# First layers of four experts made as filler and sent through memory, and all eight second layers by seven products, in an attention and expert-mixture kernel

## The chip, the cores and the metric

The kernel runs on one core of one Trainium2 chip. Its time is in device microseconds (us) of that core, and a time without further word is the median of several runs. A profiled execution has a time of its own, and its trace has a span, from the first to the last instruction, that is a little shorter. The names of the engines are PE (TensorE, matmuls), PEld (its weight loads), DVE (VectorE), ACT (ScalarE), POOL (GpSimd) and SP (SyncE, which here issues DMA transfers). SBUF is the memory on the chip that all engines work from, PSUM the small memory that matmuls write to, and DRAM stands for the large memory outside the core.

## The reference, cut to what matters

```python
# attention: 8 batches, 8 heads, 512 local and 32 global tokens, head size 64
out_g = softmax(scale * q_g @ [k_g, k_l].T) @ [v_g, v_l]
s_l   = [scale * q_l @ k_g.T, where(|i - j| <= 32, scale * q_l @ k_l.T, -1e9)]
out_l = softmax(s_l) @ [v_g, v_l]
x = concat(out_g, out_l)              # 8 * 544 = 4352 tokens, 8 * 64 = 512 columns

# routing: E = 8 experts, w_gate 512 x 8
P = exp(x @ w_gate - max)
for _ in range(8):
    P /= P.sum(1) + 1e-9              # rows
    P /= P.sum(0) + 1e-9              # columns
    P *= N / E

# experts: w1[e] 512 x 1024, w2[e] 1024 x 512; every token goes through every expert
out = sum(P[:, e:e+1] * (maximum(x @ w1[e], 0) @ w2[e]) for e in range(8))
```

The inputs and the output are fp32. P is positive, so an expert's P may be multiplied into x ahead of the first layer, into h (the result of the first layer) or into the output: the result is the same.

## The kernel before

**Tokens and groups.** The tokens stand in nine groups: m = 0 to 7 are the 512 local tokens of a batch each, m = 8 the 256 global tokens of all batches. `xT` holds the attention's output in SBUF, transposed (512 columns as 4 tiles of 128 partitions, 4352 tokens, fp16). An expert's first layer on a group is 8 blocks (FT) of 4 matmuls each, 32 matmuls of 512 columns. An expert on a group of 512 is called a unit here.

**Order.** The schedule is written out by hand: each engine does its instructions in the order in which the code issues them, and semaphores between the engines follow from the tiles. A pool with n buffers lets a new tile start when the tile n before it has been read for the last time.

**Attention.** There are 32 steps s, one for a pair of heads of a batch, worked in stages that overlap from step to step: `st_A` transposes q and k, `st_B` makes scores (L296, L298), adds the mask on DVE with its row maximum (L303) and takes the exponential on ACT (L306); `st_N` normalises (L342 and L343 on DVE, L347 on POOL), `st_D1` and `st_D2` transpose the weights (L354, L364), and `st_E` multiplies by v and copies the result into `xT` (L381). The global rows go through `st_G0` to `st_G3` in every other step; `st_G3` ends with two copies into `xT`, one on ACT and one on DVE (both L440). POOL casts q and k to fp16 (L127 for example).

**Filler.** Between these stages PE is given matmuls of experts 0 and 1. `f1(eng)` issues one first-layer block (`p_l1`: 4 matmuls, L459) and its eviction through ReLU, by ACT (L462) or DVE (L464), as `eng` says "a" or "v". `f2(eng)` issues one of the four parts of a second layer (`p_l2`: 8 matmuls, L473), its eviction (L476), and after the last one stores the unit's result y to DRAM (`yd`, L480, on ACT's queue). Both write to PSUM pool `ps_mm`, which has two buffers. A unit of group m may start at step 4m + 5. In a step from 9 on there are, in this order, two `f1("a")`, `f2("a")`, `f1("v")`, `f2("a")` and `f1("v")`, with the attention's stages between them.

**Routing.** After the last step come the routing iterations: `sk_rows` and `sk_cols` on DVE (among others two multiplications each through the helper `tt`, L698) with a sum over the partitions on PE, and filler (`tail_run`) behind each. `spread_p` then turns columns 2 to 7 of P into rows and stores them to DRAM (`pd`), from where they are loaded as `pb`, one expert's P for a group, the same on all partitions.

**Expert loop.** For each group m and each e of 2 to 7 (`egs`), `load_w1` brings w1 as fp16 (1 MB, two buffers, SP's queue, L718), `load_pb` brings pb (L725), and `scale_x` makes `xs` = x * P on DVE (L698, 128x2048). `l1` makes h (matmuls L762, eviction with ReLU on ACT L764). The second layer is done by Strassen's method for two-by-two blocks, seven products in place of eight. `prep_w2c` makes the sums of w2 blocks once for an expert: five DVE operations of 128x1024. `sums` makes those of h for each unit: one DVE operation of 128x2048 into `s` and three of 128x1024, two of them in place in `h` (L698). `product` issues products 1 to 7 of 8 matmuls of 256 columns (L798). Products 1 to 5 stay in PSUM for all experts of a group (`ps_fix`), and products 6 and 7 take a rotating buffer and are added into `o` at once (L804, DVE); after a group's last expert the five fixed ones are added too. Within one turn of the loop, PE does the products of unit i and the first layer of unit i + 1 in alternation:

```python
        for fm in range(3):
            l1(i + 1, fm, ps_rot, "r")
        for q, fm in ((3, 3), (4, 4), (5, 5), (2, 6), (1, 7), (6, None), (7, None)):
            ...
            product(i, q)
            if fm is not None:
                l1(i + 1, fm, ps_rot, "r")
```

Experts 0 and 1 come in through `load_y` (o and y1 from `yd`) and `init_o`, which multiplies them by their columns of P, four ACT operations (L750) and four DVE operations (L751) a group. The very last unit has a second layer of its own (`last_pair`, L823). `store` writes o to the output.

Of the kernel before, what the change touches and what calls it, by code (L numbers as in the profile page):

```python
# [23 lines left out]
def kernel(  # L24
# [39 lines left out]
    xT = persist.tile([P, DP, NTOK], FP16)  # L64
# [5 lines left out]
    hpool = ctx.enter_context(tc.tile_pool(name="hpool", bufs=2))  # L70
    ypool = ctx.enter_context(tc.tile_pool(name="ypool", bufs=2))
    ydram = ctx.enter_context(tc.tile_pool(name="ydram", bufs=1, space=DRAM))
    yd = [[ydram.tile([P, NJ if m < B else NT - GT0, D], FP32, name=f"yd{e}_{m}") for m in range(B + 1)]
          for e in range(2)]
    w1d = [ydram.tile([P, DP, F], FP16, name=f"w1d{e}") for e in range(2, E)]
    pd = ydram.tile([E - 2, NTOK], FP32, name="pd")

    groups = [(512 * m, 512) for m in range(B)] + [(512 * B, NTOK - 512 * B)]

# [8 lines left out]
    with tc.tile_pool(name="att_c", bufs=1) as att_c, \  # L88
# [44 lines left out]
        def load_vrow(b):  # L133
            f = vraw[b] = wpool.tile([P, H, NJ, Dh], FP32, tag="w2e", name="vraw")
            for g in range(2):
                nc.sync.dma_start(out=f[:, 4 * g : 4 * g + 4].rearrange("p h s d -> p h (s d)"),
                                  in_=v_l[b, 4 * g : 4 * g + 4].rearrange("h (p s) d -> p h (s d)", s=NJ))
# [76 lines left out]
        qgf = ypool.tile([P, H, NJ * Dh], FP32, tag="y", name="qgf")  # L214
# [151 lines left out]
        def st_E(n):  # L366
# [14 lines left out]
            cp(out=xT[:, hp, Sl * b : Sl * (b + 1)], in_=po)  # L381
# [44 lines left out]
        def st_G3(b, g):  # L426
# [10 lines left out]
            t0 = GT0 * P + Sg * b  # L437
            for a, cp in ((0, nc.scalar.copy), (1, nc.vector.tensor_copy)):
                r = slice(HB * a, HB * (a + 1))
                cp(out=xT[r, 2 * g : 2 * g + 2, t0 : t0 + Sg], in_=po[r, :, Sg * a : Sg * (a + 1)])  # L440

        def logits(t0, nt):
            pl = ps_mm.tile([P, 512], FP32, tag="mm")
            for t in range(nt):
                for dk in range(DP):
                    nc.tensor.matmul(pl[:, E * t : E * (t + 1)], xT[:, dk, P * (t0 + t) : P * (t0 + t + 1)],
# [3 lines left out]
        hTs, ysts, wts = {}, {}, {}  # L450

        def p_l1(e, m, fm, eng, pool=None, tag="mm"):
            c0, n = groups[m]
# [4 lines left out]
            for dk in range(DP):  # L458
                nc.tensor.matmul(ph[:, 0:n], wts[e][0][:, dk, P * fm : P * (fm + 1)], xT[:, dk, c0 : c0 + n],  # L459
# [5 lines left out]

        def p_l2(e, m, c, eng, pool=None, tag="mm"):
            nt = groups[m][1] // P
            if c == 0:
                ysts[(e, m)] = ypool.tile([P, NJ, D], FP32, tag="y", name="yst")
            hT, ys = hTs[(e, m)], ysts[(e, m)]  # L470
            py = (pool or ps_mm).tile([P, D], FP32, tag=tag, name="py")
            for fk in range(FT):
                nc.tensor.matmul(py, hT[:, fk, P * c : P * (c + 1)], wts[e][1][:, fk, :],  # L473
                                 start=(fk == 0), stop=(fk == FT - 1))
            if eng == "a":
                nc.scalar.copy(out=ys[:, c, :], in_=py)  # L476
            else:
                nc.vector.tensor_copy(out=ys[:, c, :], in_=py)
            if c == nt - 1:
                nc.scalar.dma_start(out=yd[e][m], in_=ys[:, 0:nt, :])  # L480

        def load_w1e(e):
            wts[e] = [wpool.tile([P, DP, F], FP16, tag="w1e", name="w1e"), None]
            nc.gpsimd.dma_start(out=wts[e][0], in_=moe_w1[e].rearrange("(dko dki) f -> dki dko f", dki=P))

        def load_w1d(e):
            nc.gpsimd.dma_start(out=w1d[e - 2], in_=moe_w1[e].rearrange("(dko dki) f -> dki dko f", dki=P))

        def load_w2e(e):
            wts[e][1] = wpool.tile([P, FT, D], FP16, tag="w2e", name="w2e")  # L490
            nc.gpsimd.dma_start(out=wts[e][1], in_=moe_w2[e].rearrange("(fko fki) d -> fki fko d", fki=P))

        fill = [(k % 2, k // 2) for k in range(2 * (B + 1))]
        n1 = n2 = 0
# [481 lines left out]
```

## Time and profile before

| | |
|---|---|
| median of three runs | 1062.13 us (1061.54 to 1063.48) |
| profiled execution, its own time | 1065.03 us |
| its span | 1063.3 us, mean granted TensorE clock 0.994 |
| PE busy | 1033.2 us, 97% of the span |
| DVE busy | 689.0 us, 65% |
| ACT busy | 550.3 us, 52% |
| POOL busy | 138.2 us, 13% |
| chain that ended last | PE 78%, ACT 11%, DVE 7%, DMA 2% |
| DMA | 160.57 MB, mean 151 GB/s |

The page of the profile gives the busy time of each engine, its share in each of 40 equal slices of the span (a digit is tenths), the chain of work that ended last, and the costliest groups of instructions: line, engine, operation, output and input tiles with their shapes, how many, then busy time and the mean of one in ns, and the idle time ahead of them with what ended it. The trace answers for a stretch of time or for single shapes in the same manner. A line of the timeline is start, duration, engine, line, operation, tiles, number of instructions, and in brackets the engine's wait ahead of it. Durations in the trace are those of one profiled execution.

### The profile page before, as it was taken

The page shows a single profiled execution, that of the slowest core. Times are in us where ns is not written, and L with a number is a line of the kernel's source. Part 1 is how long each engine was busy: PE and PEld are TensorE (multiplying, and loading weights), DVE is VectorE, ACT ScalarE, POOL GpSimd, SP SyncE. Part 2 cuts the span into 40 slices and gives each one's busy share as a digit, 9 for nine tenths or more (in the row PEclk, how much of TensorE's full clock was granted, in tenths as well). Part 3 has the DMA queues.
Part 4 walks back from the last instruction along what each step waited for, and adds up shares of the span by engine and source line. Part 5 has one row for each costly group of instructions (what it writes and reads, how often), then busy time and mean ns, then how long its engine had stood idle before and what let it go on. Part 6 is the DMA issues. An engine that isn't in the chain of part 4 may idle for free.

```text
span 1063.3 us, 20825 instructions
## 1 busy us (share of the span) xinstructions
PE 1033.2 (97%) x8444; PEld 662.8 (62%) x8444; DVE 689.0 (65%) x1443; ACT 550.3 (52%) x1340; POOL 138.2 (13%) x224
## 2 busy tenths in 40 slices
PE   7889999999999999999999999999999999999997
PEld 3555555555555456666666666666666666666686
DVE  7677667767774748776576576475484484484484
ACT  6777877878775554343343343343343343343342
POOL 6443333323414200000000000000000000000000
PEclk9999999999999999999999999999999999999999
DMA  9945786768637964534524424425326226225243
GB/s 259 213 91 150 126 205 158 124 199 166 110 99 151 234 241 156 186 111 144 187 99 141 177 100 167 151 99 191 126 100 216 101 100 218 100 100 180 93 156 117
DMA packets 95799, 160.57 MB, mean 151 GB/s; under 512 B 32716, under 2 KB 68696, under 8 KB 84696
## 3 DMA queue, kind: packets, MB, share of 16 engines
q1 hardware_dynamic: 45208, 119.98, 33.7%
q0 software_dynamic: 46736, 20.20, 15.5%
q10 hardware_dynamic: 3760, 19.07, 4.5%
q8 instruction: 66, 1.08, 0.4%
q14 instruction: 29, 0.24, 0.1%
HBM read 149.24 MB, written 33.40 MB: 172 GB/s over the span
## 4 chain that ended last, share of the span: by engine, by line
PE 78%; ACT 11%; DVE 7%; DMA 2%; issue 1%; POOL 0%; SPq 0%; ACTq 0%; DVEq 0%
PE ph L762 33%; PE m L798 20%; PE pm L798 8%; PE ph L459 6%; PE py L473 6%; ACT Pu L306 4%; ACT qbd L280 1%; ACT hT L462 1%; DVE Pu L343 1%; ACT Pg L407 1%; DVE m L404 1%; PE pv L151 1%; DMA pb<-pd 1%; DMA vraw<-in_v_l_dram 1%; ACT yst L476 1%
## 5 line engine op out<-in xcount | busy, mean ns | idle before, releaser
L764 ACT ACTIVATE h<-ph 128x512 f16<-128x512 f32 (+1 forms) x432 | 247.1, 573 | 395.3 <-PE ph L762 390.4
L762 PE MATMUL ph<-xs,w1s 128*128 128x512 f16 (+1 forms) x1728 | 405.2, 367 | 1.4 <-ACT h L764 0.5
L762 PEld LDWEIGHTS <-w1s 128*128 128x128 f16 x1728 | 169.0, 98 | 125.8 <-issue 2.6
L804 DVE SCALAR_TENSOR_TENSOR o<-pm,o 128x512 f32<-128x512 f32 (+1 forms) x106 | 70.5, 666 | 241.0 <-PE pm L798 240.7
L798 PEld LDWEIGHTS <-h 128*128 128x128 f16 x1616 | 158.1, 98 | 48.4
L798 PE MATMUL m<-w2c,s 128*128 128x256 f16 x1212 | 158.3, 273 | 0.0
L798 PEld LDWEIGHTS <-s 128*128 128x128 f16 x1212 | 118.6, 98 | 43.8
L459 PE MATMUL ph<-xT,w1e 128*128 128x512 f16 (+1 forms) x576 | 136.5, 371 | 0.0
L473 PE MATMUL py<-w2e,hT 128*128 128x512 f16 x544 | 128.4, 379 | 0.1
L698 DVE TENSOR_TENSOR xs<-xT,pb 128x2048 f16<-128x2048 f16 (+2 forms) x57 | 117.3, 2062 | 9.2 <-DMA pb<-pd 9.2
L798 PE MATMUL m<-w2c,h 128*128 128x256 f16 x808 | 105.5, 273 | 0.0
L798 PE MATMUL pm<-w2c,h 128*128 128x256 f16 x808 | 96.9, 273 | 0.0
L306 ACT ACTIVATE Pu<-ms,mx 128x160 f16<-128x160 f32 x224 | 93.6, 420 | 3.5 <-DVE mx L303 1.6
L698 DVE TENSOR_TENSOR s<-h 128x2048 f16<-128x2048 f16 (+1 forms) x106 | 92.3, 912 | 4.5 <-ACT h L764 4.5
L459 PEld LDWEIGHTS <-w1e 128*128 128x128 f16 x576 | 54.5, 100 | 48.7 <-issue 2.4
L473 PEld LDWEIGHTS <-hT 128*128 128x128 f16 x544 | 49.5, 97 | 51.3 <-issue 0.2
L303 DVE CUSTOM_DVE_ANT_0 ms<-sc,mask 128x160 f32<-128x160 f32 x224 | 60.1, 320 | 23.2 <-PE sc L298 21.8
L698 DVE TENSOR_TENSOR h<-h 128x1024 f16<-128x1024 f16 (+1 forms) x106 | 65.6, 661 | 0.0
L462 ACT ACTIVATE hT<-ph 128x512 f16<-128x512 f32 (+1 forms) x91 | 48.4, 557 | 32.4 <-PE ph L459 31.5
L804 DVE SCALAR_TENSOR_TENSOR o<-m,o 128x512 f32<-128x512 f32 (+1 forms) x90 | 52.2, 655 | 0.3
L476 ACT COPY yst<-py 128x512 f32<-128x512 f32 x68 | 39.4, 580 | 23.1 <-PE py L473 20.9
L347 POOL TENSOR_TENSOR Pl<-Pu,rs 128x256 f16<-128x256 f16 x32 | 24.2, 757 | 189.8 <-PE ph L459 53.0
(154 smaller groups left out, 1007.3 us busy)
## 6 DMA issues: line engine op xcount, KB each, us to landing
w1s<-w1d SPq DMA_DIRECT2D x54, 1024.0 KB
yd<-yst ACTq DMA_DIRECT2D x16, 1024.0 KB
pb<-pd SPq DMA_DIRECT2D x48, 256.0 KB
o<-yd SPq DMA_DIRECT2D x8, 1024.0 KB
y<-yd SPq DMA_DIRECT2D x8, 1024.0 KB
out_dram<-o SPq DMA_DIRECT2D x8, 1024.0 KB
f<-in_q_l_dram SPq DMA_DIRECT2D x15, 512.0 KB
f<-in_k_l_dram SPq DMA_DIRECT2D x15, 512.0 KB
```

The source lines that it names most:

```text
L303: nc.vector.tensor_tensor_reduce(out=ms[:, ii, :], in0=sc[:, SW * ii : SW * (ii + 1)], in1=mask[:, mi, :], scale=-scale, scalar=BIG, op0=A ...
L306: nc.scalar.activation(out=d["Pu"][:, i, :], in_=ms[:, ii, :], func=AF.Exp, scale=-1.0, bias=d["mx"][:, i : i + 1], accum_out=d["sm"][:, i ...
L347: nc.gpsimd.tensor_tensor(out=d["Pl"], in0=d["Pu"][:, :, KW:SW], in1=d["rs"].unsqueeze(2).to_broadcast([P, NHB, Sg]), op=ALU.mult)
L459: nc.tensor.matmul(ph[:, 0:n], wts[e][0][:, dk, P * fm : P * (fm + 1)], xT[:, dk, c0 : c0 + n], start=(dk == 0), stop=(dk == DP - 1))
L462: nc.scalar.activation(out=hT[:, fm, 0:n], in_=ph[:, 0:n], func=AF.Relu)
L473: nc.tensor.matmul(py, hT[:, fk, P * c : P * (c + 1)], wts[e][1][:, fk, :], start=(fk == 0), stop=(fk == FT - 1))
L476: nc.scalar.copy(out=ys[:, c, :], in_=py)
L698: nc.vector.tensor_tensor(out=out, in0=in0, in1=in1, op=op)
L762: nc.tensor.matmul(ph[:, 0:n], w1s[i][:, dk, P * fm : P * (fm + 1)], xss[i][:, dk, 0:n], start=(dk == 0), stop=(dk == DP - 1))
L764: nc.scalar.activation(out=hs[i][:, fm, 0:n], in_=ph[:, 0:n], func=AF.Relu)
L798: nc.tensor.matmul(pm[:, HD * t : HD * (t + 1)], lhs[0][:, k, lhs[1] + P * t : lhs[1] + P * (t + 1)], w[:, q - 1, k, :], start=(k == 0 and ...
L804: nc.vector.scalar_tensor_tensor(out=o, in0=pm[:, 0 : HD * nt].rearrange("p (t d) -> p t d", d=HD), scalar=sg / float(E), in1=o, op0=ALU.m ...
```

## The change

The filler makes only first layers, those of experts 0 to 3, and stores each h to DRAM (`hd`) by SP's queue. The expert loop runs over all eight experts of a group in the order 4, 0, 5, 1, 6, 2, 7, 3: an expert from 4 on is computed as before (x scaled by P on DVE, first layer, ReLU), one below 4 is loaded (`load_h`) and its h multiplied by P on POOL (`scale_h`, 128x4096 in one operation). All eight second layers go through the products. `yd`, `load_y` and `init_o` go.

Around that, `xT` becomes one tile for each group in a pool of its own, stored to DRAM (`xd`) and given back after the filler; the loop loads x for a group again (`load_x`). In the freed space the w2 blocks of experts 7 and 3 and one of the two `s` tiles are placed, so their loads are issued only after the filler. POOL prepares the w2 blocks of experts 0 to 3, DVE those of 4 to 7. `hpool` goes from 2 to 4 buffers, `ypool` from 2 to 1. `spread_p` spreads all eight columns. Each quarter of o is started by an ACT multiplication, two of them at the group's first expert and two at its end. Of the loop, a turn of even i holds the products of computed unit i with the first layer of unit i + 2 between them, and a turn of odd i the products of loaded unit i alone.

```diff
-    xT = persist.tile([P, DP, NTOK], FP16)
...
-    hpool = ctx.enter_context(tc.tile_pool(name="hpool", bufs=2))
-    ypool = ctx.enter_context(tc.tile_pool(name="ypool", bufs=2))
+    hpool = ctx.enter_context(tc.tile_pool(name="hpool", bufs=4))
+    ypool = ctx.enter_context(tc.tile_pool(name="ypool", bufs=1))
...
+    NL = E // 2
+    hd = [[ydram.tile([P, FT, n], FP16, name=f"hd{e}_{m}") for m, (_, n) in enumerate(groups)] for e in range(NL)]
+    xd = [ydram.tile([P, DP, n], FP16, name=f"xd{m}") for m, (_, n) in enumerate(groups)]
+    w1d = [ydram.tile([P, DP, F], FP16, name=f"w1d{e}") for e in range(NL, E)]
+    pd = ydram.tile([E, NTOK], FP32, name="pd")
+    psx = ExitStack()
+    xpool = psx.enter_context(tc.tile_pool(name="xpool", bufs=1, side="right"))
+    xT = [xpool.tile([P, DP, n], FP16, name=f"xT{m}") for m, (_, n) in enumerate(groups)]
...
-            cp(out=xT[:, hp, Sl * b : Sl * (b + 1)], in_=po)
+            cp(out=xT[b][:, hp, :], in_=po)
+            if hp == HP - 1:
+                nc.sync.dma_start(out=xd[b], in_=xT[b])
...
-                cp(out=xT[r, 2 * g : 2 * g + 2, t0 : t0 + Sg], in_=po[r, :, Sg * a : Sg * (a + 1)])
+                cp(out=xT[B][r, 2 * g : 2 * g + 2, t0 : t0 + Sg], in_=po[r, :, Sg * a : Sg * (a + 1)])
+            if b == B - 1 and g == 1:
+                nc.sync.dma_start(out=xd[B], in_=xT[B])
...
         def p_l1(e, m, fm, eng, pool=None, tag="mm"):
...
-                nc.tensor.matmul(ph[:, 0:n], wts[e][0][:, dk, P * fm : P * (fm + 1)], xT[:, dk, c0 : c0 + n],
+                nc.tensor.matmul(ph[:, 0:n], wts[e][:, dk, P * fm : P * (fm + 1)], xT[m][:, dk, :],
...
             if eng == "a":
                 nc.scalar.activation(out=hT[:, fm, 0:n], in_=ph[:, 0:n], func=AF.Relu)
             else:
                 nc.vector.tensor_scalar(out=hT[:, fm, 0:n], in0=ph[:, 0:n], scalar1=0.0, scalar2=None, op0=ALU.max)
+            if fm == FT - 1:
+                nc.sync.dma_start(out=hd[e][m], in_=hT[:, :, 0:n])
...
-        fill = [(k % 2, k // 2) for k in range(2 * (B + 1))]
+        fill = [(k % NL, k // NL) for k in range(NL * (B + 1))]
...
+        def f1(engs, **kw):
             nonlocal n1
-            k, fm = divmod(n1, FT)
-            if not f1_ready():
-                return 0
-            p_l1(*fill[k], fm, eng, **kw)
-            n1 += 1
-            return 1 if fill[k][1] < B else 0.5
-
-        def f2(eng, **kw):
-            nonlocal n2
-            k, c = divmod(n2, NJ)
-            need = FT * (k + 1)
-            if k >= len(fill) or n1 < need or (n1 == need and f1_ready()):
-                return 0
-            nt = groups[fill[k][1]][1] // P
-            p_l2(*fill[k], c, eng, **kw)
-            n2 += 1 if c + 1 < nt else NJ - c
-            return 2
+            v = 0
+            for eng in engs:
+                k, fm = divmod(n1, FT)
+                if k < len(fill) and slot >= HP * fill[k][1] + 5:
+                    p_l1(*fill[k], fm, eng, **kw)
+                    n1 += 1
+                    v += 1 if fill[k][1] < B else 0.5
+            return v
...
-            f1("a")
-            f1("a")
+            f1("aa")
...
             if s < NU:
                 st_B(s, 1)
-            f2("a")
+            if s > HP:
+                f1("va")
             if s + 1 < NU:
                 st_A(s + 1)
             f1("v")
...
-            f2("a")
+            if s > HP:
+                f1("va")
...
             if s > 2 * HP:
                 f1("v")
...
-    w2c = [wc.tile([P, 7, FT // 2, D // 2], FP16, name=f"w2c{e}") for e in range(2, E)]
-    y1 = wc.tile([P, NJ, D], FP32, name="y1")
+    ORDER = (4, 0, 5, 1, 6, 2, 7, 3)
+    w2c = {e: wc.tile([P, 7, FT // 2, D // 2], FP16, name=f"w2c{e}") for e in ORDER[:6]}
...
-    for e in range(2, E):
     def prep_w2c(e):
+        w = w2c[e]
+        eng = nc.gpsimd if e < NL else nc.vector
+        tt(w[:, 0], w[:, 1], w[:, 4], ALU.add, eng)
+        tt(w[:, 5], w[:, 1], w[:, 2], ALU.add, eng)
+        tt(w[:, 6], w[:, 3], w[:, 4], ALU.add, eng)
+        tt(w[:, 2], w[:, 2], w[:, 4], ALU.subtract, eng)
+        tt(w[:, 3], w[:, 3], w[:, 1], ALU.subtract, eng)
+
+    for e in ORDER[:6]:
         load_w2c(e)
...
+    def load_x(m):
+        if m <= B:
+            xgs[m] = xsp.tile([P, DP, 512], FP16, tag="xg", name="xg")
+            nc.sync.dma_start(out=xgs[m][:, :, 0 : groups[m][1]], in_=xd[m])
...
+    def alloc_h(i):
+        if i < NUN:
+            hs[i] = hpool.tile([P, FT, 512], FP16, tag="hT", name="h")
+
+    def load_h(i):
+        if i < NUN:
+            m, e = units[i]
+            alloc_h(i)
+            nc.sync.dma_start(out=hs[i][:, :, 0 : groups[m][1]], in_=hd[e][m])
+
+    def scale_h(i):
+        if i < NUN:
+            n = groups[units[i][0]][1]
+            h = hs[i][:, :, 0:n]
+            tt(h, h, pbs.pop(i)[:, 0:n].unsqueeze(1).to_broadcast([P, FT, n]), ALU.mult, nc.gpsimd)
...
-        s = ss[i] = wpool.tile([P, 3, HF, 256], FP16, tag="w2e", name="s")
+        s = ss[i] = (wpool.tile([P, 3, HF, 256], FP16, tag="w2e", name="s", bufs=1) if i % 2 else
+                     wr.tile([P, 3, HF, 256], FP16, tag="s", name="s"))
...
+    def closes(i):
+        m, e = units[i]
+        return e == (ORDER[-1] if m < B else ORDER[-2])
...
+    def add(i, q, pm):
+        m, e = units[i]
+        nt = groups[m][1] // P // 2
+        if m not in os_:
+            os_[m] = ypool.tile([P, NJ, D], FP32, tag="y", name="o")
+        for j, (r, d, sg) in enumerate(QUARTER[q]):
+            o = os_[m][:, nt * r : nt * (r + 1), HD * d : HD * (d + 1)]
+            p = pm[:, 0 : HD * nt].rearrange("p (t d) -> p t d", d=HD)
+            if (q >= 6 and e == ORDER[0]) or (q in (3, 4) and j == 0):
+                nc.scalar.mul(o, p, 1.0 / float(E))
+            else:
+                nc.vector.scalar_tensor_tensor(out=o, in0=p, scalar=sg / float(E), in1=o, op0=ALU.mult, op1=ALU.add)
...
+        pt = ps_po.tile([P, 3, P], FP32, tag="po", name="pt")
+        pts = xsp.tile([3 * NT, 3, P], FP32, tag="xs", name="pts")
+        parts = [(k, 3 * k, min(3 * k + 3, E)) for k in (1, 0, 2)]
+        for k, e0, e1 in parts:
+            nc.tensor.matmul(pt[0 : (e1 - e0) * NT, k, :], lt[:, e0:e1, :], idf, start=True, stop=True)
+            nc.scalar.mul(pts[0 : (e1 - e0) * NT, k], pt[0 : (e1 - e0) * NT, k], float(E))
+            nc.sync.dma_start(out=pd[e0:e1].rearrange("e (t p) -> (e t) p", p=P), in_=pts[0 : (e1 - e0) * NT, k, :])
...
+    load_pb(0)
+    load_x(0)
     load_w1(0)
-    load_pb(0)
     load_pb(1)
-    prep_w2c(2)
-    prep_w2c(3)
+    prep_w2c(4)
+    prep_w2c(0)
+    prep_w2c(1)
     scale_x(0)
-    scale_x(1)
+    load_pb(2)
+    scale_x(2)
     tail_run(1000)
-    load_w1(1)
-    load_pb(2)
-    load_y(0)
+    load_w1(2)
+    psx.close()
+    wr = ctx.enter_context(tc.tile_pool(name="wr", bufs=1, side="right", reuse_waits="tile"))
+    for e in ORDER[6:]:
+        w2c[e] = wr.tile([P, 7, FT // 2, D // 2], FP16, name=f"w2c{e}")
+        load_w2c(e)
+    alloc_h(0)
+    load_h(1)
+    scale_h(1)
     for fm in range(FT):
         pool, tag = cyc[fm % 2]
         l1(0, fm, pool, tag)
+    sums(0)
...
+    for i, (m, e) in enumerate(units):
+        if i == NUN - 1:
             last_pair(i)
-            break
-        sums(i)
-        if e == 2 and i > 0:
-            init_o(m)
-        scale_x(i + 2)
-        if m == 0 and e + 2 < E:
-            prep_w2c(e + 2)
-        for fm in range(3):
-            l1(i + 1, fm, ps_rot, "r")
-        for q, fm in ((3, 3), (4, 4), (5, 5), (2, 6), (1, 7), (6, None), (7, None)):
-            if i == 0 and q == 2:
-                init_o(m)
-            product(i, q)
-            if fm is not None:
-                l1(i + 1, fm, ps_rot, "r")
+        elif i % 2 == 0:
+            alloc_h(i + 2)
+            load_pb(i + 3)
+            load_pb(i + 4)
+            if (i + 4) % E == 0:
+                load_x((i + 4) // E)
+            load_h(i + 3)
+            load_w1(i + 4)
+            scale_h(i + 3)
+            for fm in range(3):
+                l1(i + 2, fm, ps_rot, "r")
+            for q, fm in ((3, 3), (4, 4), (5, 5), (2, 6), (1, 7), (6, None), (7, None)):
+                product(i, q)
+                if fm is not None:
+                    l1(i + 2, fm, ps_rot, "r")
+                if q == 3:
+                    if i + 2 < NUN:
+                        sums(i + 1)
+                    else:
+                        n = groups[m][1]
+                        h = hs[i + 1]
+                        s = ss[i + 1] = wpool.tile([P, HF, n], FP16, tag="w2e", name="sl", bufs=1)
+                        tt(s, h[:, 0:HF, 0:n], h[:, HF:FT, 0:n], ALU.add)
+                if q == 4:
+                    scale_x(i + 4)
+                if q == 5 and m == 0 and i + 2 < E:
+                    prep_w2c(units[i + 2][1])
+                    if i + 3 > 3:
+                        prep_w2c(units[i + 3][1])
+            if closes(i):
+                for q in (3, 4, 5, 2, 1):
+                    add(i, q, fixed[q])
+        else:
+            if i + 1 < NUN:
+                sums(i + 1)
+            for q in (3, 4, 5, 2, 1, 6, 7):
+                product(i, q)
+                if closes(i) and q in (3, 4):
+                    add(i, q, fixed[q])
+            if closes(i):
+                for q in (5, 2, 1):
+                    add(i, q, fixed[q])
+                store(m)
```

## Prediction, written before the result was known

> **What bounds the kernel now.** I read the page's busy table first, then the chain of waits in the last two thirds, the groups by shape, and the timeline of single steps of the first third.
>
> The page:
>
> ```profile
> PE 1033.2 (97%) x8444; PEld 662.8 (62%) x8444; DVE 689.0 (65%) x1443; ACT 550.3 (52%) x1340; POOL 138.2 (13%) x224
> ...
> POOL 6443333323414200000000000000000000000000
> ```
>
> TensorE (PE) never rests for long, and POOL does nothing after the first third. The chain of waits inside the expert loop (start, us, what):
>
> ```profile
> 448.58 1.75 PE pm L798 x16
> 450.33 2.59 PE ph L762 x12
> 452.92 0.87 PE m L798 x8
> 453.79 0.86 PE ph L762 x4
> ...
> 461.60 1.75 PE pm L798 x16
> ```
>
> One unit (an expert on 512 tokens) takes 461.60 - 448.58 = 13.02 us and the chain is PE alone. A 512-column matmul costs 2.59 / 12 = 0.216 us, a 256-column one 0.875 / 8 = 0.109 us: first layer 32 x 0.216 = 6.91, second layer 7 products x 0.875 = 6.12. So the loop is bound by PE and only matmuls taken away shorten it, as long as everything else stays hidden.
>
> The groups by shape (busy, mean ns) give VectorE's (DVE's) prices:
>
> ```profile
> L698 DVE TENSOR_TENSOR xs<-xT,pb 128x2048 f16<-128x2048 f16 x47 | 107.5, 2286 | 0.4 <-DMA pb<-pd 0.4
> L804 DVE SCALAR_TENSOR_TENSOR o<-pm,o 128x512 f32<-128x512 f32 x96 | 66.3, 691 | 231.1 <-PE pm L798 231.0
> L698 DVE TENSOR_TENSOR h<-h 128x1024 f16<-128x1024 f16 x96 | 61.8, 686 | 0.0
> L698 DVE TENSOR_TENSOR s<-h 128x2048 f16<-128x2048 f16 x48 | 58.3, 1215 | 4.5 <-ACT h L764 4.5
> L464 DVE TENSOR_SCALAR hT<-ph 128x512 f16<-128x512 f32 x53 | 36.6, 691 | 16.6 <-PE ph L459 16.2
> ```
>
> The timeline of DVE and POOL near the start:
>
> ```profile
> 22.55 0.96 DVE L343 TENSOR_TENSOR Pu<-Pu,rs 128x768 f16<-128x768 f16 x1
> ...
> 27.15 1.05 POOL L127 CAST ks<-f 128x1024 f16<-128x1024 f32 x1
> 27.70 1.33 DVE L343 TENSOR_TENSOR Pu<-Pu,rs 128x768 f16<-128x768 f16 x1
> 28.14 1.78 POOL L196 CAST gs<-kgf 64x1024 f16<-64x1024 f32 x1
> ...
> 236.51 0.61 POOL L347 TENSOR_TENSOR Pl<-Pu,rs 128x256 f16<-128x256 f16 x1 [8.90 <-DVE Pu L343]
> ```
>
> This is the row I hang most on. L343 has two operands in SBUF; 30 of its 32 large forms take 0.96 us. The two that meet a POOL cast take longer: the one at 27.70 ends 0.83 after the cast ahead of it, and the next cast, 1.04 elsewhere, takes 1.78 and ends 0.89 after L343. They exclude each other. DVE operations with one operand in PSUM (L303: 0.319 us beside POOL, 0.320 without) do not.
>
> **The change, part by part.** All against the profiled execution: span 1063.3, its own time 1065.03, 2.9 above the median of 1062.13; I add the sum to the median.
>
> *Second layers of two experts by products.* 17 units of 512 tokens (2 experts x 8.5 groups) go from 32 x 0.216 = 6.91 to 6.12: 17 x 0.785 = -13.3 us on PE. First layers are as many as before, 34 units as filler and 34 in the loop, so nothing else leaves PE.
>
> *Filler.* Each attention step had four first-layer groups (0.86 us each) and two second-layer groups (1.73); now it has eight first-layer groups. PE work is equal, ACT still evicts four, DVE evicts four where it had two: +2 x 0.69 per step of 10.24. DVE is 70% busy there, so the sum fits; the place doesn't. The step's last three groups are v, a, v by evicting engine, and the pool `ps_mm` has two buffers: the last group may not start until DVE has evicted the first of the three, and on DVE that eviction stands behind L343 and, in every other step, behind the L440 copy, which waits for ACT. Two steps of the timeline:
>
> ```profile
> 161.01 1.90 PE L473 MATMUL py<-w2e,hT 128*128 128x512 f16 x8
> 161.65 0.96 DVE L343 TENSOR_TENSOR Pu<-Pu,rs 128x768 f16<-128x768 f16 x1
> 162.75 1.03 PE L459 MATMUL ph<-xT,w1e 128*128 128x512 f16 x4
> ...
> 171.62 1.89 PE L473 MATMUL py<-w2e,hT 128*128 128x512 f16 x8
> 173.34 1.03 PE L459 MATMUL ph<-xT,w1e 128*128 128x512 f16 x4
> 173.82 0.23 DVE L440 CAST xT<-pog 64x64 f16<-64x64 f32 x1 [0.91 <-ACT xT L440]
> ```
>
> In the first, DVE is free at 162.61, evicts until 163.32, and PE's group moves from 162.75 to 163.37: 0.62. In the second DVE is free at 174.05, evicts until 174.76, and the group moves from 173.34 to 174.81: 1.47, less the 0.22 that PE waits at L354 anyway. Twelve steps of each kind (9 to 32): 12 x 0.62 + 12 x 1.25 = 22.4. Against it, steps 5 to 8 now hold 28 groups where they held the equal of 20, and their 5.7 us of idle PE takes some up: 2.4. I take +20 (8 if later steps drift into slack, 24 at most). The 34 stores of h go through the SP queue; the store of an h waits for evictions of its own step, and the loads behind it are for a later one: 0.
>
> *Scaling loaded h on POOL.* 128x4096, two operands, no row like it. L347 (two operands, 256 elements) takes 0.61 undisturbed: 9.7 us scaled up whole, 8.3 with 0.1 fixed; a one-operand cast (1.04 for 1024) would give 4.2. I take 9.0, between the two-operand values. Two pages of the Trainium skill speak against this change. GPSIMD Engine Reference (Performance versus the Vector engine) gives 4497 ns for a two-input fp32 operation of 2048 elements, which doubled is an estimate of 9.0 us; its engine-selection table sends such work to VectorE. SBUF — State Buffer (Who interferes with whom) says that POOL and a DVE instruction with two SBUF inputs hold a shared port pair for a whole instruction. The trace shows that only for instructions of 1 us. By the pages' 9.0 the sum is the 1118 below.
>
> By the one-operand row, 4.2, the two engines' two-operand work would come to 13.0 of a pair's 19.17 and, in the first group, to 84.9 of PE's 94 (both are made up below): nothing would be held, and the sum would be the second rival's 1069.
>
> Per pair of units PE needs 6.91 + 2 x 6.12 = 19.17. DVE's two-operand work is two sums (1.215 + 3 x 0.686 = 3.27 each) and one scaling of x (2.29): 8.83. With POOL's 9.0 that makes 17.8, 1.3 under PE. If nothing else ran beside POOL, the 2.76 of adds would come on top, 20.6 a pair, and 4.1 of extra adds at each group's end: 86.5 a group against 76.7. In the built order POOL's h waits only for the products of a computed unit some units back, so POOL can run ahead and find its place. I take +1 a group, 7.5 groups: +8 (0 to +74). SP's load of pb is queued behind POOL's last scaling, with the loads of h and w1 behind it; both are used a pair later: 0.
>
> *First group.* Here POOL also prepares w2 of four experts, 20 operations of 1024 elements, 2.25 each (a quarter of 9.0), ten before the loop and ten in its first group. From the end of the routing iterations I reckon with six early ones left: POOL 6 x 2.25 + four h 36.0 + ten 22.5 = 72.0. DVE in the same stretch: four preparations of 3.4 (five of 0.683), five x scalings 11.4, eight sums 26.2 = 51.3. Excluding each other, 123. PE needs 10.4 (filler left) + 6.9 + 76.7 = 94.0. Difference 29; w2 loads of the last two experts stand between on POOL's queue (eight issues of 0.75 = 6), and 3 for waits at hand-overs: +38 (20 if DVE's adds and waits cover more, 50 if all ten early ones are left).
>
> *Routing iterations.* DVE's chain there leaves PE 0.2 us an iteration. Early preparations meet two or three of them, two multiplies each, about 1.3 an iteration: +3 (0 to 6). Initialising o (L750, L751) goes, but was hidden.
>
> Sum: -13.3 + 20 + 8 + 38 + 3 = +55.7, so 1062.1 + 55.7 = 1118.
>
> **Rivals.**
>
> *PE stays the bound (the other side).* Place: every wait for DVE, in filler and loop. If DVE is held up for less than 13.3 us in all, the saving lands; if for nothing, 1062.1 - 13.3 = 1049. For it: DVE is only 65% busy, and the exclusion rests on two meetings of short instructions. Against it: the filler stall alone is 20, from buffers and order, and would have to fall below 0.55 a step.
>
> *No exclusion for long instructions.* POOL reads in pieces and DVE slips in. The last three terms go: 1062.1 - 13.3 + 20 = 1069. For: no POOL instruction above 1.9 us in the trace. Against: both engines waited to the end of the other's instruction.
>
> *Exclusion bounds the loop throughout.* POOL starts just before the sums in every pair: 7.5 x 9.8 = 74 in place of 8, 1184. It decides above about 10.3 us a scaling (19.17 - 8.83), or below it where the order falls badly.
>
> That the products are not made for all eight experts can be left out: the built order has 56 per unit in all eight.
>
> **How the numbers follow.** Forecast 0.73 (1077 to 1160, from the low ends, -13.3 + 8 + 20, and the high ends of all but the steady loop with about 31 of its 74), no exclusion 0.10, exclusion throughout 0.09, PE bound 0.06, cancelling 0.02. The range takes in no exclusion and leaves the outer two: 1068 to 1160. 0.2% (2 us) is about what a measurement of this kernel can tell. Faster 0.06, same 0.02, slower 0.92.
>
> **What would show it.** Right: the scaling of h at 8 to 10 us on POOL; sums and x scalings on DVE far above 1.2 and 2.3 us where they meet it; PE waiting for DVE at the first-layer line in filler steps of about 11.2 us; a first group near 115, later ones near 78. Wrong: steps still at 10.24, DVE's rows unchanged beside POOL, or every group at 86.

## The result, and the profile after

The changed kernel takes 1212.03 us (four runs, 1209.05 to 1213.22) against 1062.70 before: a ratio of 1.140, 95% interval 1.138 to 1.143. It is slower, as forecast, but by 149 us where 56 were forecast, and the range (1068 to 1160) did not hold the time. The profiled execution took 1209.05 us, its span is 1207.3, its mean granted clock 0.947 where it was 0.994.

The page's busy times and three of its rows of 40 slices:

```profile
PE 1048.1 (87%) x8854; PEld 709.9 (59%) x8854; DVE 929.8 (77%) x1506; ACT 478.5 (40%) x1220; POOL 481.1 (40%) x286
...
PE   7798998998999285849799799798998998998978
...
POOL 7341342233123914980532542452432524325412
PEclk9999999999999697879899899899998998998999
```

PE, which never rested, has a hole in slice 14 (digit 2), weak slices in the first group behind it, and then a lower digit in about every third slice (30 us): one place in each group. In the hole POOL shows a 9, and the granted clock falls wherever PE has a low digit.

The spans of both executions, cut at the same places (start of the last of the 32 stages `st_D1`, which transpose weights, first matmul of the loop's first layers, first product, first store, end):

| stretch | before | after | more | predicted |
|---|---|---|---|---|
| attention with filler | 327.7 | 351.5 | +23.8 | +20 |
| routing, to the loop's first layer | 62.5 | 82.9 | +20.4 | +3 |
| first layer to first product | 10.5 | 13.7 | +3.2 | in the next |
| loop | 662.6 | 759.2 | +96.6 | +32.7 |
| span | 1063.3 | 1207.3 | +144.0 | +55.7 |

The loop's first product to the store of the first group takes 121.0 us, the next stores stand 85.2, 84.9, 85.3, 85.0, 85.0, 85.1 and 81.5 apart, and the last half group takes 46.1. PE would need 76.7 a group. So the first group loses 44.3, the seven next ones 55.2, the last 7.8, together 107.3; the products' saving is the other part of the +96.6. For the eighth group and the last half the need is a little lower: with one store moved (below) they take 72.8 and 37.3.

The groups by shape (busy, mean ns, then idle ahead of them):

```profile
L675 POOL TENSOR_TENSOR h<-h,pb 128x4096 f16<-128x4096 f16 x32 | 273.0, 8532 | 407.0 <-DMA h<-hd 330.6 <-DVE s L675 39.9 <-ACT h L742 18.5
L675 DVE TENSOR_TENSOR h<-h 128x1024 f16<-128x1024 f16 x128 | 189.4, 1519 | 0.0
L675 POOL TENSOR_TENSOR w2c<-w2c 128x1024 f16<-128x1024 f16 x20 | 48.7, 2469 | 0.0
```

The scaling on POOL is 8.0 us where nothing is in its way (9.0 was taken), a preparation 2.1 (2.25 taken). DVE's sums of 0.69 us have a mean of 1.52: the two engines do hold each other up.

### The profile page after: what moved, and what is told of

Same layout as the page of the kernel before. It is cut to its first block, busy times and chain, and to the rows that moved or that the text cites. A ratio compares the mean times of both kernels' runs of the same rounds, so it can differ in the third digit from the quotient of the medians.

```text
span 1207.3 us, 21811 instructions
## 1 busy us (share of the span) xinstructions
PE 1048.1 (87%) x8854; PEld 709.9 (59%) x8854; DVE 929.8 (77%) x1506; ACT 478.5 (40%) x1220; POOL 481.1 (40%) x286
## 3 DMA queue, kind: packets, MB, share of 16 engines
q10 hardware_dynamic: 1168, 1.25, 0.4%
## 4 chain that ended last, share of the span: by engine, by line
PE 63%; DVE 16%; ACT 9%; issue 6%; DMA 3%; POOL 2%; SPq 1%; DVEq 0%; ACTq 0%; POOLq 0%
PE m L783 23%; PE ph L740 18%; PE ph L466 10%; PE pm L783 9%; ACT Pu L309 4%; DVE h L675 3%; DVE w2c L675 2%; DVE hT L471 2%; DVE lg L675 2%; ACT hT L469 2%; DVE o L800 1%; DVE Pu L346 1%; ACT qbd L283 1%; DVE s L675 1%; DVE m L409 1%
## 5 line engine op out<-in xcount | busy, mean ns | idle before, releaser
L675 POOL TENSOR_TENSOR h<-h,pb 128x4096 f16<-128x4096 f16 (+1 forms) x36 | 289.7, 8047 | 453.1 <-DMA h<-hd 371.6
L742 ACT ACTIVATE h<-ph 128x512 f16<-128x512 f32 (+1 forms) x288 | 164.8, 573 | 548.2 <-PE ph L740 530.7
L740 PE MATMUL ph<-xs,w1s 128*128 128x512 f16 (+1 forms) x1152 | 290.9, 387 | 73.1 <-DVE o L800 61.7
L466 PE MATMUL ph<-xT,w1e 128*128 128x512 f16 (+1 forms) x1152 | 262.0, 370 | 20.9 <-DVE hT L471 20.6
L783 PEld LDWEIGHTS <-h 128*128 128x128 f16 x2160 | 214.0, 99 | 67.4 <-issue 22.9
L675 DVE TENSOR_TENSOR s<-h 128x1024 f16<-128x1024 f16 (+2 forms) x142 | 194.2, 1408 | 13.8 <-POOL h L675 8.0
L675 DVE TENSOR_TENSOR h<-h 128x1024 f16<-128x1024 f16 (+1 forms) x142 | 198.6, 1438 | 0.0
L466 PEld LDWEIGHTS <-w1e 128*128 128x128 f16 x1152 | 107.5, 99 | 121.9 <-issue 29.8
L675 DVE TENSOR_TENSOR xs<-xg,pb 128x2048 f16<-128x2048 f16 (+1 forms) x36 | 79.8, 2218 | 56.9 <-DMA pb<-pd 41.2
L471 DVE TENSOR_SCALAR hT<-ph 128x512 f16<-128x512 f32 x109 | 75.3, 690 | 25.9 <-PE ph L466 24.7
L309 ACT ACTIVATE Pu<-ms,mx 128x160 f16<-128x160 f32 x224 | 93.6, 421 | 4.0 <-DVE mx L306 2.3
```

Of the source, the lines that this page charges most:

```text
L309: nc.scalar.activation(out=d["Pu"][:, i, :], in_=ms[:, ii, :], func=AF.Exp, scale=-1.0, bias=d["mx"][:, i : i + 1], accum_out=d["sm"][:, i ...
L466: nc.tensor.matmul(ph[:, 0:n], wts[e][:, dk, P * fm : P * (fm + 1)], xT[m][:, dk, :], start=(dk == 0), stop=(dk == DP - 1))
L471: nc.vector.tensor_scalar(out=hT[:, fm, 0:n], in0=ph[:, 0:n], scalar1=0.0, scalar2=None, op0=ALU.max)
L675: (eng or nc.vector).tensor_tensor(out=out, in0=in0, in1=in1, op=op)
L740: nc.tensor.matmul(ph[:, 0:n], w1s[i][:, dk, P * fm : P * (fm + 1)], xss[i][:, dk, 0:n], start=(dk == 0), stop=(dk == DP - 1))
L742: nc.scalar.activation(out=hs[i][:, fm, 0:n], in_=ph[:, 0:n], func=AF.Relu)
```

## The experiments

Before ran beside each; its medians were 1061.3 to 1062.9. Times below are medians of four runs. The start of the attention alone differs by up to 3.8 us between profiled executions of the same code (the tenth `st_D1` starts at 108.6 to 112.4), so stages are compared by their lengths.

**Where the routing lost 20 us.** In the timeline of the changed kernel, DVE's last multiplication of the routing and POOL's preparations of experts 0 and 1:

```profile
395.36 21.36 DVE L675 TENSOR_TENSOR lg<-lg,cr 128x272 f32<-128x272 f32 x1
...
395.66 20.76 POOL L675 TENSOR_TENSOR w2c<-w2c 128x1024 f16<-128x1024 f16 x10
```

The multiplication, 0.44 us in the other iterations, ends 0.3 us after the tenth preparation. P can't leave for memory before that, and PE waits 21.5 us for its copy (L862).

```diff
-        eng = nc.gpsimd if e < NL else nc.vector
+        eng = nc.vector
```

> The changed kernel with one line altered: all w2 preparations on VectorE, none on POOL; the scaling of h stays on POOL. Theory (VectorE's two-operand work and POOL's exclude each other): the last routing multiplication, 21.4 us in the changed kernel, falls to 0.44, the first layer of unit 0 starts about 20 us earlier (434 to 414), and the first group loses some 10 to 20 us of its 121 between first product and store; in all 1212 - 35 = 1177 us, between 1165 and 1187. Rival (the late start came from the w2 loads or from P's way through memory, and POOL's preparations were beside it): 1203 to 1215, and the first layer starts past 425. The groups after the first stay at 85 us in both.

Measured: 1181.39 us (ratio 1.113, 1.111 to 1.115). The theory holds: P is copied out 44 us after the last transposing stage where it was 65, the first group takes 100.5 in place of 121.0, the later ones stay at 84.7 to 86.3. Of the 21 us a part returned: the first layer now waits 8.7 us for w1, and the first product comes 19.1 after it, not 13.7.

In a later run the same row of preparations was started a little later instead, behind one POOL copy that reads P:

```diff
+    nc.gpsimd.tensor_copy(out=gate, in_=lg[:, 0, 0:1])
     prep_w2c(4)
     prep_w2c(0)
```

> The changed kernel with one GpSimd copy of a single column of P ahead of its ten early preparations, so that they begin when the last routing multiplication has ended, about a microsecond later than in the change. Theory (only that multiplication was kept out by the whole row; elsewhere the engines take turns): it takes 0.44 us, P goes to memory 20 us earlier, VectorE's five preparations of expert 4 meet the row and take 2 to 3 us each, the first layer begins near 421 as with all preparations on VectorE, 1212 - 13 = 1199 (1192 to 1204). Rival (a row of GpSimd instructions keeps out whatever VectorE operation meets it): the five preparations wait until about 417 and x is scaled near 431 again, 1206 to 1214.

Measured: 1198.29 us (1.129, 1.127 to 1.131). In its timeline:

```profile
395.53 0.44 DVE L675 TENSOR_TENSOR lg<-lg,cr 128x272 f32<-128x272 f32 x1
396.01 0.40 DVE L862 COPY lt<-lg 128x272 f32<-128x272 f32 x1
396.32 10.79 DVE L675 TENSOR_TENSOR w2c<-w2c 128x1024 f16<-128x1024 f16 x5
...
396.43 25.08 POOL L675 TENSOR_TENSOR w2c<-w2c 128x1024 f16<-128x1024 f16 x10
```

Against the same row DVE's five preparations have their turns: 10.79 us where 3.09 is their time alone, and POOL's ten take 25.08 for 20.76. The time saved is that of the one multiplication, less what came late next.

**Turns or keeping out.** A run put the ten preparations into the middle of the routing, where they meet many multiplications.

```diff
-    for e in ORDER[:6]:
+    for e in (0, 1):
+        load_w2c(e)
+    for e in (0, 1):
+        prep_w2c(e)
+    for e in (4, 5, 6, 2):
         load_w2c(e)
```

> The changed kernel with GpSimd's ten early preparations (experts 0 and 1) moved ahead of the w2 loads of 4, 5, 6 and 2 on its queue, so that they run back to back in the middle of the routing iterations and not at their end. Theory (turns: a VectorE multiplication waits for the GpSimd instruction that is running, 2.1 us at most, and then has its turn): some ten routing multiplications of 0.44 us take 1 to 2.5 us each, none takes 10, the iterations are 8 to 15 us longer in all, and 1212 becomes 1200 to 1212. Rival (kept out: a fp32 multiplication that meets a row of GpSimd instructions waits for all of them): one multiplication takes up to 21 us and the other fifteen 0.44, so that the time is near 1212 again, 1207 to 1217.

Measured: 1216.12 us (1.145, 1.143 to 1.147). The mechanism came out as the theory says, the time did not. Four multiplications in DVE's timeline:

```profile
373.33 2.40 DVE L675 TENSOR_TENSOR lg<-lg,cr 128x272 f32<-128x272 f32 x1
378.65 1.90 DVE L675 TENSOR_TENSOR lg<-lg,rs 128x272 f32<-128x272 f32 x1
...
385.27 1.90 DVE L675 TENSOR_TENSOR lg<-lg,rs 128x272 f32<-128x272 f32 x1
388.76 0.69 DVE L675 TENSOR_TENSOR lg<-lg,cr 128x272 f32<-128x272 f32 x1
```

No multiplication takes more than 2.4 us, and the way to P's copy is 9.8 us shorter. But the w2 loads of experts 4, 5, 6 and 2 now stand behind the preparations on POOL's queue; the first product comes 26.3 us after the first layer where it came 13.7, and the gain is gone. What PE waits for there is w1, 8.65 us ahead of the first layer and 4.97 us within it; that the late w2 loads hold w1 up is argued, not shown. That the loads would be late was overlooked in the expectation.

**Where each group lost 8.4 us.** One place in a group of the changed kernel, in the timelines of SP, DVE, POOL and PE:

```profile
796.06 0.42 SPq L696 DMA_DIRECT2D w1s<-w1d  x1
824.60 0.39 SPq L803 DMA_DIRECT2D out_dram<-o  x1
825.09 1.52 SPq L703 DMA_DIRECT2D pb<-pd  x2
...
803.01 9.11 DVE L675 TENSOR_TENSOR h<-h 128x1024 f16<-128x1024 f16 x2
...
832.32 2.29 DVE L675 TENSOR_TENSOR xs<-xg,pb 128x2048 f16<-128x2048 f16 x1 [4.81 <-DMA pb<-pd]
834.52 9.61 DVE L675 TENSOR_TENSOR s<-h 128x2048 f16<-128x2048 f16 x2
...
802.73 8.24 POOL L675 TENSOR_TENSOR h<-h,pb 128x4096 f16<-128x4096 f16 x1 [10.29 <-DMA h<-hd]
834.89 8.70 POOL L675 TENSOR_TENSOR h<-h,pb 128x4096 f16<-128x4096 f16 x1 [23.92 <-DMA h<-hd]
...
838.74 1.03 PE L740 MATMUL ph<-xs,w1s 128*128 128x512 f16 x4
845.99 3.57 PE L740 MATMUL ph<-xs,w1s 128*128 128x512 f16 x8 [6.23 <-DVE o L800]
849.36 1.52 PE L783 MATMUL m<-w2c,h 128*128 128x256 f16 x8
```

SP works its queue in order, and the store of the finished group stands ahead of pb and waits for the group's last addition. So SP issues nothing from 796.5 to 824.60, although the two buffers of pb were free at 810.97 (end of POOL's scaling) and 814.32 (end of the last x scaling). Then the store goes, the two pb behind it at 825.09 and 825.63, 14 and 11 us after their buffers were free, and they are there 7 us later. So DVE's x scaling is late and POOL's scaling begins 0.4 us after DVE's sums have; the second part of the sums waits for POOL. The additions behind it on DVE's queue are late, no PSUM buffer of `ps_rot` comes free, and PE stands for 6.23 us. Then it restarts slowly: the next 8 matmuls take 849.36 - 845.99 = 3.37 us instead of 1.73, the 8 behind them 1.36 instead of 0.87. 6.23 + 1.64 + 0.49 = 8.36, which is the 85.1 - 76.7 of a group. The other three pairs of the group run at PE's pace, although in two of them a sum waits out a scaling too (803.01 is one); the six groups after the first are alike in this.

```diff
-                store(m)
+                late = m
...
             load_w1(i + 4)
+            if late is not None:
+                store(late)
+                late = None
```

> The changed kernel with the store of a finished group issued by SP behind the next turn's loads in place of ahead of them. In the changed kernel each group after the first loses 8.4 us in one place: SP issues the store, pb lands 7 us later, the scaling of x is late, POOL's scaling of h begins ahead of the sums of the loaded unit, and VectorE's sums and the adds behind them wait 8.7 us. Theory (it is this order that makes the collision): the groups fall from 85.1 to about 77, 7.5 x 8 = 60 us, 1152 us (1145 to 1170). Rival (POOL's scaling collides with something in every group, wherever it begins; with 17.8 of 19.2 us a pair taken there is no room): the loss moves and the groups stay above 83, 1195 to 1215.

Measured: 1141.26 us (1.075, 1.073 to 1.076), a little under the expected range's low end: the place of one store on SP's queue was worth 71 us. The six groups after the first are at 76.5 to 76.9, PE's own time. The turn's loads now go out ahead of the store, the two pb as soon as their buffers are free (785.08 and 787.83). The engines still meet in each group, as the timelines of SP, POOL and DVE show:

```profile
785.08 3.07 SPq L703 DMA_DIRECT2D pb<-pd  x2
...
798.08 0.39 SPq L803 DMA_DIRECT2D out_dram<-o  x1
...
776.90 8.15 POOL L675 TENSOR_TENSOR h<-h,pb 128x4096 f16<-128x4096 f16 x1 [8.16 <-DMA h<-hd]
...
777.11 8.49 DVE L675 TENSOR_TENSOR h<-h 128x1024 f16<-128x1024 f16 x1
```

A sum's last operation waits out the whole scaling here as well, but at a place where PE needs nothing from DVE for that long. So it is the place of the meeting that costs, not its being there.

A second test of the same thing cut the scaling into pieces:

```diff
+            for k in range(FT):
+                tt(h[:, k], h[:, k], pb[:, 0:n], ALU.mult, nc.gpsimd)
```

> The changed kernel with the scaling of h on GpSimd in eight operations of 128x512 in place of one of 128x4096. Theory (the two engines exclude each other by the instruction, and take turns at its end): a VectorE operation waits 1.1 us at most, the four of a sum 4.4 in place of 8.7; the groups fall from 85.1 to about 81, 1212 - 30 = 1182 (1170 to 1195). Rival (GpSimd keeps VectorE out as long as it has instructions queued, as with the ten preparations in a row at 395.7 to 416.4): groups at 85 or above, 1205 to 1225.

Measured: 1184.32 us (1.115, 1.113 to 1.117), inside the theory's range, though in part by luck. DVE's operations have turns between the pieces: two sums that meet them take 3.22 us together, where one waited 8.49. But the groups after the first stand 81.7 to 84.8 apart, 83 on average where 81 was expected, and 8.4 us of the gain come from the first group, which the sum left out.

**Without POOL.** All of the new work on DVE, with the preparations' line changed as in the first run, and the scaling called at the end of an odd turn in place of the top of an even one:

```diff
-            tt(h, h, pbs.pop(i)[:, 0:n].unsqueeze(1).to_broadcast([P, FT, n]), ALU.mult, nc.gpsimd)
+            tt(h, h, pbs.pop(i)[:, 0:n].unsqueeze(1).to_broadcast([P, FT, n]), ALU.mult)
...
-            scale_h(i + 3)
...
+            scale_h(i + 2)
```

> The changed kernel with all preparations and the scaling of h on VectorE; the scaling stands at the end of the turn before the unit's sums, so that its load has landed. Theory (all but the filler's loss comes from POOL and VectorE excluding each other): VectorE's work of a pair of units is 8.8 + 4.6 + 2.8 = 16.2 us of PE's 19.2, groups are at 77, the first one at 85 to 95; 1212 - 20 (routing) - 35 (first group) - 60 (later groups) = 1097 us (1080 to 1110). Rival (loads through memory, or PE's clock, hold the loop back): groups stay above 80 with PE waiting for loads, above 1120.

Measured: 1112.72 us (1.046, 1.042 to 1.050), just above the range. Later groups are at 76.5 to 77.3 as expected. The groups by shape show that DVE does a scaling in half of POOL's time:

```profile
L675 DVE TENSOR_TENSOR h<-h,pb 128x4096 f16<-128x4096 f16 x32 | 141.3, 4415 | 0.0
```

Two terms of the sum were smaller than expected. The start gave 11 us in place of 20, since the first product comes 19.1 us after the first layer where it came 13.7; the first group became 28.8 us shorter in place of 35, though its 92.2 are in the range given. In this run the store still stands ahead of the loads, and the last half group takes about 45 us where it takes 37.3 with the store moved; there PE waits 5.3 us for w1. The run with both earlier mends and the scaling left on POOL comes to the same time:

> The changed kernel with both: all preparations on VectorE, and the store of a group behind the next turn's loads; the scaling of h stays on GpSimd. Theory (they are separate losses): 1212 - 31 - 71 = 1110, between 1104 and 1117, with the groups after the first at 76.5. Rival (they share a cause, the phase of GpSimd's scaling, or the sooner start moves the scalings against the sums again): above 1120, or groups above 80.

Measured: 1112.73 us (1.046, 1.043 to 1.050). The two losses add up, 1212 - 31 - 71 = 1110. With the queue in order, POOL's 8 us a pair cost nothing after the first group, which takes about 101 us here.

**The filler.** In the timeline of the changed kernel PE waits in each step for DVE's eviction of the block two before, as predicted:

```profile
208.02 1.02 PE L466 MATMUL ph<-xT,w1e 128*128 128x512 f16 x4 [1.42 <-DVE hT L471]
...
217.81 1.02 PE L466 MATMUL ph<-xT,w1e 128*128 128x512 f16 x4 [0.35 <-DVE hT L471]
```

First try: the second `f1("va")` as `f1("av")`, so that ACT evicts that block.

> The changed kernel with the second f1("va") of a step written f1("av"), so that ACT evicts the block two before the step's last one. Theory (PE's last block of a step waits for VectorE's eviction of the block two before, which is queued behind L346 or the L445 copy): the pair of steps falls from 21.9 us to about 20.5, some 24 x 0.8 = 19 us in all, 1193 us (1187 to 1200). Rival (VectorE has too much to do in a step, wherever the eviction stands): within 4 us of 1212.

Measured: 1213.54 us (1.144, 1.141 to 1.147), no gain. In PE's timeline the wait changes its owner:

```profile
210.76 1.02 PE L466 MATMUL ph<-xT,w1e 128*128 128x512 f16 x4 [0.93 <-ACT hT L469]
```

ACT too has work of the attention ahead of the eviction. Second try: the block itself is moved ahead of `st_N`, so that its eviction stands ahead of the normalisation on DVE.

```diff
+            if s > HP:
+                f1("v")
             if s < NU:
                 st_N(s, 0, 6)
...
-                f1("va")
+                f1("a")
```

> The changed kernel with the first block of the second f1("va") moved ahead of st_N, so that on VectorE its eviction stands before L346 in place of behind it; engines of the evictions as in the change. Theory (the block two before the step's last one is evicted late because its eviction is queued behind the normalisation): the pair of steps falls from 21.9 us to 20.5 to 20.8, 24 x 0.6 to 0.8 = 14 to 19 us, 1193 to 1198. Rival (three blocks in a row on two PSUM buffers wait for whatever evicts them, as the moved letter showed): 1207 to 1214.

Measured: 1198.47 us (1.128, 1.126 to 1.130). A pair of steps falls from 21.9 to 20.84, and the attention ends 11.9 us sooner, of which 11.0 lie between the tenth and the last `st_D1` (224.7 us before, 242.5 in the changed kernel, 231.5 here). So about half of the filler's +23.8 was this order. In that stretch PE waited 19.1 us for DVE's evictions in the changed kernel; here it waits 0.2 for DVE's and 8.0 for ACT's, so most of the other half is the wait for ACT.

**Together.** All mends, and w2 loads of experts 6 and 2 held back until P had been through memory:

> All of it together: preparations on VectorE behind the additions of their turn, the store behind the loads, the early eviction in the filler, and the w2 loads of experts 6 and 2 issued only when P has been through memory; the scaling of h stays on GpSimd. If the early eviction works: 1110 - 16 - 8 (earlier first layer) - 10 (first group) = 1076; if not, 1092. Rival (the collisions of scaling and sums in the first group remain): 1095 to 1110. Before was 1062; none of these reaches it.

Measured: 1097.29 us (1.032, 1.031 to 1.034), the rival's range. The first layer begins at 397.6 and stands still from 401 to 409.8, since ACT waits for the buffer of h(0), whose last store is queued on SP behind loads that wait for the scaling of x; the first group takes 99. The next run changed that order, put four preparations ahead of the loop, the last four w2 loads behind h(1), and the scalings of the first group on DVE:

> The run with everything together, mended at the start: preparations on VectorE, four of them ahead of the loop; scaling of h on VectorE in the first group and on GpSimd after; the store behind the loads; the early eviction; the last stores of h ahead of what waits for P on SP's queue; the w2 loads of the last four experts behind the first h. In the run before it the first layer began at 398 but the first product at 427, and the first group took 99 us. Theory (the start is held by ACT waiting for the store of the filler's last h, and the first group by VectorE's preparations and GpSimd's scalings excluding each other): first product by 412, first group at 82 to 88, 1097 - 15 - 13 = 1069, between 1060 and 1080; about the 1062 of before and not clearly under it. Rival (the start is held by DMA that is full): first product after 420, 1080 to 1095.

Measured: 1081.07 us (1.017, 1.014 to 1.020), a microsecond over the theory's range. The start came out as expected (first product at 412.3); the first group, 95.8 to its store, is not as short as hoped. One more scaling on DVE:

> The run with everything together, mended at the start, with the first scaling of h of the second group also on VectorE, so that GpSimd begins one pair of units later. In that run GpSimd's first scaling began 0.3 us after a sum of the loaded unit was issued, the sum took 9.6 us, and PE waited 8.3 us. Theory (that meeting is what is left in the first group): 1081 - 8 = 1073 (1069 to 1077). Rival (the first scaling on GpSimd meets a sum wherever it begins, or VectorE has too much to do in the first group): 1078 to 1084. Before: 1061; the difference that stays is the filler's.

Measured: 1077.56 us (1.015, 1.013 to 1.017), between theory and rival. This is the fastest version that was found, and it is slower than before. From the third on, its groups are at 76.5 with the clock at 1.00, so the saving by the products is there in full; the first group, 93.6 to its store, and 13 us of filler outweigh it.

## Why the prediction was wrong, point by point

*The saving* is real: 78.1 us a group became 76.5 in every run whose queues were in order.

*The filler* was right in place and size: +23.8 for +20, in waits of 0.35 and 1.42 us where 0.62 and 1.25 were predicted; they come to 20.6 us where the working has 22.4.

*The routing* failed: "+3 (0 to 6)" was made of short meetings with early preparations spread over the iterations. They came as ten in a row at the end, because the w2 loads ahead of them on POOL's queue end only then, and one multiplication waited for all of them: 20.9 us.

*The first group*: 44.3 and 3.2 for 38 are in the bounds given, but that is luck in part. The term starts at the end of the routing iterations and reckons with six early preparations left; all ten were, and they stood ahead of P itself instead of running beside PE's work. Counted from there, with the 20.4 of the routing, the two terms took 67.9 for 41, and 56 was their most. That the two engines exclude each other in the first group was right: it fell from 121.0 to 100.5 without POOL's preparations and to 92.2 without POOL. What keeps it over PE's 76.7 even then stays open.

*The steady loop* failed, and is the largest part: "+1 a group" against 8.4 in each of the six groups after the first; the eighth and the last half lose 8.7 and 8.8 against the run with the store moved. That POOL can find a place beside the sums was right, as the 76.5 of the reordered store shows. The step that failed is the one on SP's queue: "SP's load of pb is queued behind POOL's last scaling ... both are used a pair later: 0". The store ahead of pb was not followed. It keeps SP from issuing the two pb for 14 and 11 us after their buffers are free, they need another 7 to be there, and the delay turns a meeting that was free into one that holds PE. With the store behind the loads the six groups are at 76.5 to 76.9.

*The clock* was left out. A wait of PE costs its length and a slow restart. In the stretch behind the 6.23 us wait, the windows of the trace show (us, busy times of PE, PEld, DVE, ACT, POOL, then granted clock, DMA share, GB/s):

```profile
846.00:850.00 4.00, 4.00 (x11) 1.57 (x11) 4.00 (x6) 1.00 (x2) 0.00 (x0) 0.50 0.97 343
850.00:853.00 3.00, 3.00 (x21) 2.06 (x20) 1.68 (x1) 0.80 (x2) 1.73 (x1) 0.94 0.58 246
```

The clock is at half for some 4 us, which made 8.4 of 6.2. The Trainium skill has this (TensorE: Matmul & The Clock Gate, Part 1: The HAM clock gate): half the rate after an idle window of about 3.4 us, and full rate after about as long of work. The trace agrees as far as it goes: 0.50 for 4 us behind a wait of 6.23 us, and 1.00 throughout the filler (160 to 318), where no wait is over 1.5 us.

*The rivals.* "Exclusion bounds the loop throughout" came nearest in time (1184) but not in mechanism: it wants PE held in every pair. A sum waited out a scaling in three of the four pairs of a group, and PE was held by one of them. "No exclusion" (1069) is out: 8.49 us for a sum of 0.69. The Trainium skill's rule of the port pair held for a whole instruction (SBUF — State Buffer, Who interferes with whom) holds here for instructions of 8 us too.

## What to carry to other kernels

When two engines exclude each other, their summed time says little; look for what puts the one just ahead of the other's urgent work, and follow every entry of every queue up to it, stores of finished results among them. A store that waits for its data holds up everything behind it on its queue, so a load that the next step needs goes ahead of a store for which nobody waits. Price a wait of PE of some 6 us at its length and the slow restart.

## What the runs showed of the hardware that was not expected

At the boundary between two POOL instructions, even back to back, a waiting DVE operation gets its turn: between the eight pieces of a scaling (two sums in 3.22 us), and five times in a row against ten preparations (10.79 us). There is one exception that the runs do not explain. In the changed kernel and in the four other runs with that order, the last routing multiplication was kept out through nine such boundaries (20.0 to 21.5 us), although the same kind of multiplication had its turns in the middle of the routing. Which engine began first doesn't explain it: in the changed kernel the multiplication began 0.3 us ahead of the row, in three of the others about 1 us behind its start. What differs there stays open.
